# Sinkhorn normalisation of two batches with one row or column per partition, and the other two batches' chain placed later

## The chip, the core and the metric

The kernel runs on one core of a Trainium2 chip. Its metric is the device time of one execution in microseconds; three runs were taken, and one more execution was profiled. Engines are named as in the profile: PE (TensorE, the matrix engine), DVE (VectorE), ACT (ScalarE), POOL (GpSimd) and SP (SyncE, which here only starts DMAs).

## The reference

Four batches, 8 heads, 768 positions, head dimension 64. Each sequence is cut into 8 blocks of 96. A small 8 x 8 matrix per batch and head (`sort_net`) is turned into a soft permutation by five rounds of exp, division by row sums and division by column sums (Sinkhorn). It mixes the blocks of k and v; attention then runs block by block, and the result goes through a feed-forward network with squared ReLU.

```python
for _ in range(5):
    P = P - np.max(P, axis=-1, keepdims=True)
    P = np.exp(P)
    P = P / (np.sum(P, axis=-1, keepdims=True) + 1e-09)
    P = P / (np.sum(P, axis=-2, keepdims=True) + 1e-09)
k_sorted = np.einsum('bhij,bhjcd->bhicd', P, k_b)     # v the same way
scores = scale * np.matmul(q_b, k_sb.transpose(0, 1, 2, 4, 3))
attn = softmax(scores)                                # over the 96 keys of one block
x = np.matmul(attn, v_sb)                             # (3072 tokens, 512)
h = np.maximum(x @ w_in, 0.0)                         # 512 -> 2048
out = h * h @ w_out                                   # 2048 -> 512
```

## The kernel before

**Order.** Nothing is left to a scheduler of the framework. The kernel lists its operations in a planner (`Plan`), each with an engine, a cost in microseconds and what it depends on; `Plan.run` plays the list through in time, and the operations are issued on each engine in the order in which they began there. Each engine then works strictly in that order. On PE there are two lists, attention and feed-forward; an attention operation is taken when it is ready before the next feed-forward piece, or when its due number (the table `DUES`, counted in feed-forward pieces) has come. `FIRST` is the order of batch 0's first half, written by hand: K, V (sorting k, v), S (scores), T (turning v), A (attention times v), X (turning the output), F (first pieces of the feed-forward); an upper-case letter evicts on ACT, a lower-case one on DVE. The costs and dues of the planner are constants in the kernel.

**Sinkhorn.** `p_sb` holds the 32 matrices (4 batches x 8 heads), one per partition, 64 numbers each. One iteration is an exp on ACT (L465) and six DVE instructions: reduce, reciprocal and multiply along rows, and the same along columns (L409 to L416). After the fifth, `p_last` multiplies once more into bf16 and transposes 32 x 32 (L424), and `p_spread` (L489) multiplies with a 0/1 matrix `sel`, so that each partition (j, c) holds P[i, j] of every head. `build_w` (L501) multiplies this with a 0/1 mask into `w_all`, the 128 x 128 weights with which k and v are sorted on PE (`s_sort`, L628; for the second halves of batch 0 `s_sort2`, L664). Some further small instructions on `xT` (L448, L452, L456) run each kind of instruction once, and their results are not used. While PE has nothing to do in this stage, `fill` (L438) gives it matmuls on `ones`.

**The rest.** Batch 0 is done in two halves, so that feed-forward work can begin early. Batches 1 to 3 sort k and v in another layout, by small matmuls with `w_t` (`build_wt`, L526 and L533; `s_nat`, L784), which needs P of all batches. V goes through DRAM and back (`v_way`, L808 and L814). Scores are L699, their exp L719 and L728, attention times v L890, its normalisation L900 and L901. Each feed-forward unit takes 384 tokens: 16 groups of four matmuls up (L1012), ReLU on ACT (L1020), square on DVE (L1023), and 48 matmuls down in groups of four (L1042).

**Loads.** POOL issues nearly all of them (L324): q of batch 0 (heads 4 to 7), k and v of batch 0 by pairs of heads, `w_in` in four parts, `w_out` in four parts, then v, k and q of batch 1. SP issues the other half of batch 0's q (`q32`, as fp32, cast on ACT at L473), and ACT `sort_net`. POOL also builds the identity, the masks and a part of `w_all` between its loads.

Of the kernel before, what the change touches and what calls it, by code (L numbers as in the profile page):

```python
# [8 lines left out]
FP32 = mybir.dt.float32  # L9
# [12 lines left out]
    (0, "K"): (-242.5, -237.0, -449.5, -391.0),  # L22
    (0, "S"): (-214.5, -217.0, -359.5, -370.5),
    (0, "T"): (-167.5, -226.5, -373.0, -268.5),
    (0, "A"): (-159.0, -195.0, -306.0, -99.0),
    (0, "X"): (-124.0, -130.5, -290.5, -94.5),
    (0, "W"): (-245.5,),
    (1, "V"): (-115.0, -110.5),
    (1, "Q"): (-94.0,),
    (1, "N"): (None, -50.5),  # L30
    (1, "Z"): (None, None, 33.5, 34.0),
    (1, "S"): (-53.0, -3.0, 38.5, 51.0),
    (1, "A"): (-45.5, 3.5, 45.5, 51.0),
    (1, "X"): (43.5, 24.5, 56.0, 53.5),
    (2, "L"): (60.0,),
    (2, "N"): (66.5, 69.5),
    (2, "V"): (63.5, 79.5),
    (2, "Z"): (77.5, 81.5, 85.5, 81.5),
    (2, "S"): (80.0, 84.0, 102.5, 97.0),
    (2, "A"): (82.0, 86.0, 102.5, 98.0),  # L40
    (2, "X"): (90.5, 118.0, 111.0, 114.0),
    (3, "L"): (123.0,),
    (3, "N"): (132.0, 141.0),
    (3, "V"): (128.0, 138.5),
    (3, "Z"): (133.5, 133.5, 149.5, 143.0),
    (3, "S"): (147.0, 153.0, 161.0, 158.0),
    (3, "A"): (147.0, 154.5, 162.0, 158.5),
    (3, "X"): (156.5, 161.5, 195.0, 182.0),
# [4 lines left out]
FIRST = ("K0' v0 K1 v1 S0 t0' S1 t1' A0 K2' V2 A1 K3 S2 t2' v3' S3 x1' A2 T3' x0 A3 X2' F1 F0 "  # L53
         "F4 F3 F7 F6 X3")
# [130 lines left out]
def kernel(  # L185
# [60 lines left out]
    def copy(eng, out, in_):  # L246
        if eng == "ACT":
            nc.scalar.copy(out=out, in_=in_)  # L248
        else:
# [14 lines left out]
    p_sb = const.tile([NH, NB, NB], FP32)  # L264
    nc.scalar.dma_start(out=p_sb, in_=sort_net.rearrange("b h i j -> (b h) i j"))
    xT = const.tile([128, d_model // 128, B * S], BF16)
    q32 = [xT[:, 1 + g, 2 * S:].bitcast(FP32).rearrange("p (h x) -> p h x", h=2)
           for g in range(2)]
    for g in range(2):
        nc.sync.dma_start(out=q32[g], in_=q_r[0, :, 2 * g:2 * g + 2, :])  # L270
# [5 lines left out]
    nc.vector.memset(ident, 0.0)  # L276

# [35 lines left out]
    w_out_bf = const.tile([128, NT, d_model], BF16)  # L313
    w_all = const.tile([128, H + HP, NB, C0], BF16)
# [6 lines left out]
    def dma(key, mb, dst_src, deps=(), long=True, rate=0.23):  # L321
        def issue(e):
            dst, src = dst_src()
            nc.gpsimd.dma_start(out=dst, in_=src)  # L324
        op = plan.add("POOL", 0.75, issue, deps)
        landed[key] = plan.add("DMA", mb / (0.39 if key[0] == 0 else 0.43 if long else rate), lambda e: None, [op, landed.get("last")])
        landed["last"] = landed[key]
# [25 lines left out]
    first = plan.add("DMA", 3.95, lambda e: None)  # L353
# [3 lines left out]
    id_op = plan.add("POOL", 0.4, lambda e: make_identity(nc, ident, nomemset=True))  # L357
# [41 lines left out]
    rs = const.tile([NH, NB], FP32)  # L399
    cs = const.tile([NH, NB], FP32)  # L400
    pf = const.tile([NH, NB, NB], BF16)
    sel = xT[0:32, 0, 3 * S:3 * S + 32 * C0].rearrange("p (j c) -> p j c", c=C0)
    pt = const.tile([128, NB, NH], BF16)
    p_ij = const.tile([NH, 2, NH], BF16)

    def sink_norm(e, axis, last=False):
        view = p_sb if axis == 0 else p_sb.transpose([0, 2, 1])
        r = rs if axis == 0 else cs
        nc.vector.reduce_sum(out=r, in_=view, axis=AX.X)  # L409
        nc.vector.reciprocal(out=r, in_=r)  # L410
        if last:
            return
        nc.vector.tensor_tensor(
            out=p_sb, in0=p_sb,
            in1=(r[:, :, None] if axis == 0 else r[:, None, :]).to_broadcast([NH, NB, NB]),
            op=ALU.mult)  # L416

    def p_last(e, k):

        i = slice(NQ * k, NQ * (k + 1))  # L420
        nc.vector.tensor_tensor(
            out=pf[:, i, :], in0=p_sb[:, i, :],
            in1=cs[:, None, :].to_broadcast([NH, NQ, NB]), op=ALU.mult)
        nc.vector.transpose(out=p_ij[:, k, :],  # L424
                            in_=pf[:, i, :].rearrange("h i j -> h (i j)"))
# [16 lines left out]
    t32 = xT[:, 3, 2 * S:].bitcast(FP32)  # L442
    nc.vector.memset(t32[:, 0:136], 1.0)

    def warm(e):
        fill(2.4, 0)
        for n in range(2):
            nc.tensor.matmul(out=p2[1][:, 0, 8 * n:8 * n + 8], lhsT=t32[:, 0:128],  # L448
                             rhs=t32[:, 128:136], start=True, stop=True)

    def try_exp(e):
        nc.scalar.activation(out=t32[:, 144:152], in_=t32[:, 128:136], func=AF.Exp,  # L452
                             accum_out=t32[:, 152:153])

    def try_rec(e):
        nc.vector.reciprocal(out=t32[:, 160:168], in_=p2[1][:, 0, 8:16])  # L456


    plan.add("PE", 4.3, warm, [plan.add("DVE", 1.1, lambda e: None)])

    exps, casts = [], []
    step = plan.add("SP", 2.25, lambda e: None)
    step0 = step
    for it in range(5):
# [3 lines left out]
        if it == 0:  # L468
            plan.add("ACT", 0.3, try_exp, [step])
# [750 lines left out]
```

## Time and profile before

| | |
|---|---|
| median of three runs | 219.02 us (218.44 to 220.64) |
| the profiled execution | 218.59 us, of which 216.8 us between first and last instruction |
| granted PE clock, mean | 0.998 |
| PE busy | 209.8 us, 97% of the span |
| DVE, ACT, POOL busy | 109.9, 121.4, 28.4 us |
| HBM read, written | 29.70 MB, 8.72 MB |
| matmuls up, L1012 | 506, 88.1 us |
| matmuls down, L1042 | 368, 84.6 us |

The span is cut by the profile into 40 slices of 5.4 us; digits give the busy share of an engine in tenths. Matmuls overlap and their ends are modelled, so PE's share is not a share of peak. The chain of work that ended last is followed back from the last instruction, each step to what released it. A line number is that of the kernel printed above; one line can hold the copies of many stages (L248 on ACT, L250 on DVE).

### The profile page before, as it was taken

How to read it: one execution, taken by the hardware profiler on the slowest of the kernel's cores; microseconds unless marked ns; L12 is line 12 of the kernel's file. 1: busy time of each engine (PE TensorE's matmuls, PEld its weight loads, DVE VectorE, ACT ScalarE, POOL GpSimd, SP SyncE). 2: the span in 40 equal slices, each digit the busy share in tenths (PEclk: the TensorE clock that was granted, in tenths of full speed). 3: DMA queues.
4: the chain of work that ended last, by engine and by line, in shares of the span. 5: the costliest groups of instructions: out<-in, count | busy, mean ns of one | idle time of the engine just before them, and what ended most of it. 6: DMA issues, size and time to landing. Idle time of an engine off the chain costs nothing.

```text
span 216.8 us, 5097 instructions
## 1 busy us (share of the span) xinstructions
PE 209.8 (97%) x2040; PEld 116.1 (54%) x2040; DVE 109.9 (51%) x300; ACT 121.4 (56%) x252; POOL 28.4 (13%) x53
## 2 busy tenths in 40 slices
PE   8898999799999999999999999999999999999994
PEld 3466765346655555445665455445655565456542
DVE  4778576345894447643895045517675154015300
ACT  5777985227783268436774177328865375147421
POOL 7994320000000700000000330000000000000000
PEclk9999999999999999999999999999999999999999
DMA  6999999999968799939852599599884310120012
GB/s 183 194 204 207 206 208 209 194 173 292 225 125 76 136 211 228 188 102 194 187 153 64 121 192 215 105 208 229 98 209 115 91 48 3 48 97 0 0 51 97
DMA packets 47864, 31.92 MB, mean 147 GB/s; under 512 B 27296, under 2 KB 42912, under 8 KB 47840
## 3 DMA queue, kind: packets, MB, share of 16 engines
q1 hardware_dynamic: 35568, 18.34, 37.8%
q0 software_dynamic: 12224, 13.24, 37.8%
q8 instruction: 16, 0.26, 0.5%
q14 instruction: 8, 0.07, 0.1%
q10 hardware_dynamic: 48, 0.01, 0.0%
HBM read 29.70 MB, written 8.72 MB: 177 GB/s over the span
## 4 chain that ended last, share of the span: by engine, by line
PE 81%; DMA 14%; POOL 3%; issue 1%; ACT 0%; POOLq 0%
PE op L1042 36%; PE hp L1012 34%; DMA vb<-in_v_dram 9%; DMA w_in_bf<-in_moe_w_in_dram 5%; PE p L890 3%; PE p L699 3%; PE p L784 2%; PE op L1070 2%; POOL vb L324 1%; POOL kb L324 1%; POOL qb L324 1%; PE qtp L578 0%; PE p L628 0%; PE xtp L943 0%; POOL ident masks.py:199 0%
## 5 line engine op out<-in xcount | busy, mean ns | idle before, releaser
L1012 PE MATMUL hp<-xT,w_in_bf 128*128 128x384 bf16 x506 | 88.1, 326 | 0.0
L1042 PE MATMUL op<-w_out_bf,h 128*128 128x512 bf16 x368 | 84.6, 379 | 0.0
L1020 ACT ACTIVATE h<-hp 128x384 bf16<-128x384 f32 x128 | 61.7, 495 | 17.8 <-PE hp L1012 14.7
L1023 DVE TENSOR_TENSOR h<-h 128x384 bf16<-128x384 bf16 x128 | 43.6, 354 | 44.2 <-ACT h L1020 43.8
L1012 PEld LDWEIGHTS <-w_in_bf 128*128 128x128 bf16 x506 | 47.3, 98 | 31.2 <-issue 0.7
L1042 PEld LDWEIGHTS <-h 128*128 128x128 bf16 x368 | 33.9, 98 | 38.3 <-issue 1.2
L248 ACT COPY ob<-op 128x512 f32<-128x512 f32 (+2 forms) x23 | 13.1, 568 | 48.7 <-PE op L1042 46.3
L728 ACT ACTIVATE et<-p 96x384 bf16<-96x384 f32 x48 | 19.7, 488 | 9.3 <-PE p L699 9.3
L901 DVE TENSOR_TENSOR ao<-p,rec 96x512 bf16<-96x512 f32 x32 | 22.0, 686 | 1.3 <-DVE rec L900 0.2
L890 PEld LDWEIGHTS <-et 96*128 96x128 bf16 x256 | 11.7, 97 | 5.2 <-issue 0.7
L250 DVE CAST vn<-p 128x768 bf16<-128x768 f32 x6 | 5.7, 958 | 15.1 <-PE p L784 10.7
L900 DVE RECIPROCAL rec<-p 96x8 f32<-96x8 f32 x32 | 6.4, 201 | 10.3 <-PE p L890 8.7
L1159 POOL COPY held<-xT 1x3 bf16<-1x3 bf16 (+1 forms) x2 | 0.4, 186 | 85.8 <-DMA xT<-ao 85.8
L248 ACT CAST vn<-p 128x768 bf16<-128x768 f32 x6 | 4.8, 800 | 9.1 <-PE p L784 9.1
L890 PE MATMUL p<-vblk,et 96*128 96x65 bf16 x192 | 9.6, 193 | 0.0
L438 PE MATMUL p<-ones 128*128 128x512 bf16 (+1 forms) x28 | 8.5, 433 | 1.1 <-DVE ones L274 1.1
L699 PEld LDWEIGHTS <-kvT 64*128 64x128 bf16 x256 | 6.2, 94 | 5.4 <-issue 3.1
L844 DVE COPY kvT<-kx 128x768 bf16<-128x768 bf16 x10 | 8.4, 847 | 0.0
L250 DVE CAST kn<-p 128x768 bf16<-128x768 f32 x5 | 4.8, 956 | 5.5 <-PE p L784 5.5
L324 POOL DMA_DIRECT2D kb<-in_k_dram x10 | 6.5, 646 | 4.1 <-DMA w_out_bf<-in_moe_w_out_dram 1.8
L324 POOL DMA_DIRECT2D vb<-in_v_dram x10 | 6.3, 630 | 3.0 <-DMA w_in_bf<-in_moe_w_in_dram 3.0
L324 POOL DMA_DIRECT2D qb<-in_q_dram x8 | 6.0, 750 | 2.7 <-DMA w_in_bf<-in_moe_w_in_dram 1.9
(88 smaller groups left out, 120.0 us busy)
## 6 DMA issues: line engine op xcount, KB each, us to landing
out_dram<-ob SPq DMA_DIRECT2D x23, 256.0 KB, 3.2
v_way<-vn SPq DMA_DIRECT2D x6, 396.0 KB, 5.3
vblk<-v_way SPq DMA_DIRECT2D x6, 396.0 KB, 4.1
vb<-in_v_dram POOLq DMA_DIRECT2D x6, 384.0 KB, 11.9
kb<-in_k_dram POOLq DMA_DIRECT2D x6, 384.0 KB, 10.4
qb<-in_q_dram POOLq DMA_DIRECT2D x6, 384.0 KB, 13.4
w_in_bf<-in_moe_w_in_dram POOLq DMA_DIRECT2D x4, 512.0 KB, 11.1
w_out_bf<-in_moe_w_out_dram POOLq DMA_DIRECT2D x4, 512.0 KB, 16.3
```

Of the source, the lines that this page charges most:

```text
L248: nc.scalar.copy(out=out, in_=in_)
L250: nc.vector.tensor_copy(out=out, in_=in_)
L324: nc.gpsimd.dma_start(out=dst, in_=src)
L438: nc.tensor.matmul(out=p2[slot][:, 0, 0:128 * r].rearrange("p (r x) -> p r x", r=r), lhsT=ones, rhs=ones[:, None, :].to_broadcast([128, r, ...
L699: nc.tensor.matmul(out=scp[:, h, BLK * n:BLK * (n + 1)], lhsT=u.ksT[64 * h:64 * (h + 1), HS * hf + BLK * n:HS * hf + BLK * n + 128], rhs=( ...
L728: nc.scalar.activation(out=et[:, h, 0:HS].rearrange("p (n c a) -> p n c a", c=C0, a=NA), in_=st["p"][0:96, h, 0:HS].rearrange("p (n a c) - ...
L890: nc.tensor.matmul(out=oup[:, h, 66 * n:66 * n + D + 1], lhsT=et_r[u.et[hf]][:, h, BLK * n:BLK * n + 128], rhs=(u.vs[:, NQ * hf + n, h, 0: ...
L901: nc.vector.tensor_tensor(out=u.ao[:, n0:n0 + NQ, :, :].rearrange("p n e d -> p e n d"), in0=ov[:, :, :, 0:D], in1=rec[:, :, :, None].to_b ...
L1012: nc.tensor.matmul(out=t["hp", nt][:, 0:HS], lhsT=w_in_bf[:, kc, 128 * nt:128 * (nt + 1)], rhs=xT[:, kc, t0:t0 + HS], start=(kc == 0), sto ...
L1020: nc.scalar.activation(out=t["h1", nt], in_=t["hp", nt][:, 0:HS], func=AF.Relu)
L1023: nc.vector.tensor_tensor(out=t["h2"][:, nt, :], in0=t["h1", nt], in1=t["h1", nt], op=ALU.mult)
L1042: nc.tensor.matmul(out=t["op", mt], lhsT=t["h2"][:, nt, 128 * mt:128 * (mt + 1)], rhs=w_out_bf[:, nt, :], start=(nt == 0), stop=(nt == NT ...
```

## The change

The two first batches (16 heads, 128 rows of 8) get a tile of their own, `p_a`, with one matrix row per partition. The row sum of the first iteration comes with the exp (`accum_out`). `widen` writes the normalised rows as a block-diagonal 128 x 128 matrix, and an fp32 matmul with `by_i` turns it: from there on a partition holds a column. In iterations 1 to 4 the exp takes the column's reciprocal as its scale; an fp32 matmul with the block matrix `blk` adds the rows up over partitions; `by_columns` multiplies by the reciprocal and gives the column sum in the same instruction. At the end one bf16 matmul with `spread` takes the place of transposes and eight small matmuls, and both first `w_all` builds read its PSUM tile.

The last two batches keep the old form on 16 partitions (`p_sb`, `late_norm`), five iterations issued one by one among the feed-forward work, and `late_spread` puts them into `pt` ahead of `build_wt`. `sort_net` is now loaded by SP, `p_a` first, then `q32`, then `p_sb`. `make_identity` stands ahead of the first loads on POOL; the unused instructions are gone; the fill ahead of the chain is shorter. `pt` holds heads and rows in the other order. `DUES`, `FIRST`, the engines of the first query copies and the planner's numbers for loads are set anew.

```diff
-FIRST = ("K0' v0 K1 v1 S0 t0' S1 t1' A0 K2' V2 A1 K3 S2 t2' v3' S3 x1' A2 T3' x0 A3 X2' F1 F0 "
-         "F4 F3 F7 F6 X3")
+FIRST = ("k0' V0 k1 V1 S0 t0' S1 t1' A0 K2 V2' A1 K3 S2 t2' v3 S3 X0 A2 T3' X1' X2' A3 F0 F1 F3 "
+         "F4 F6 F7 x3")
...
-    p_sb = const.tile([NH, NB, NB], FP32)
-    nc.scalar.dma_start(out=p_sb, in_=sort_net.rearrange("b h i j -> (b h) i j"))
+    p_a = const.tile([128, NB], FP32)
+    nc.sync.dma_start(out=p_a, in_=sort_net[0:HA // H].rearrange("b h i j -> (b h i) j"))
...
+    make_identity(nc, ident, nomemset=True)
...
+    for g in range(2):
+        nc.sync.dma_start(out=q32[g], in_=q_r[0, :, 2 * g:2 * g + 2, :])
+    p_sb = const.tile([HL, NB, NB], FP32)
+    nc.sync.dma_start(out=p_sb, in_=sort_net[HA // H:].rearrange("b h i j -> (b h) i j"))
...
+    def widen(dst, src, r):
+        nc.vector.scalar_tensor_tensor(
+            out=dst.rearrange("p (h i) -> p h i", i=NB),
+            in0=src[:, None, :].to_broadcast([128, HA, NB]), scalar=r,
+            in1=by_h[:, :, None].to_broadcast([128, HA, NB]), op0=ALU.mult, op1=ALU.mult)
+
+    def by_columns(src, with_):
+        nc.vector.scalar_tensor_tensor(
+            out=ph, in0=src, scalar=1.0, in1=with_, op0=ALU.mult, op1=ALU.mult,
+            accum_out=sums[:, 2:3])
+        nc.vector.reciprocal(out=sums[:, 3:4], in_=sums[:, 2:3])
...
     def warm(e):
-        fill(2.4, 0)
-        for n in range(2):
-            nc.tensor.matmul(out=p2[1][:, 0, 8 * n:8 * n + 8], lhsT=t32[:, 0:128],
-                             rhs=t32[:, 128:136], start=True, stop=True)
+        fill(1.7, 0)
...
+    def chain_step(it):
+        if it == 0:
...
+            exps.append(plan.add("ACT", 0.3, lambda e: nc.scalar.activation(
+                out=e_a, in_=p_a, func=AF.Exp, accum_out=sums[:, 0:1]), [step]))
+            def rows(e):
+                nc.vector.reciprocal(out=sums[:, 1:2], in_=sums[:, 0:1])
+                widen(wide, e_a, sums[:, 1:2])
...
+                nc.tensor.matmul(out=chain["p"][:, 0, :], lhsT=wide, rhs=by_i,
+                                 start=True, stop=True)
...
+            chain["ph"] = plan.add("DVE", 0.48, lambda e: by_columns(chain["p"][:, 0, :], one8), [pe])
+        else:
+            exps.append(plan.add("ACT", 0.2, lambda e: nc.scalar.activation(
+                out=e_a, in_=ph, func=AF.Exp, scale=sums[:, 3:4]), [chain["ph"]]))
+            pe = plan.add("PE", 0.22, lambda e: nc.tensor.matmul(
+                out=chain["p"][:, it, :], lhsT=blk, rhs=e_a, start=True, stop=True), exps[-1:])
+            def norm(e):
+                nc.vector.reciprocal(out=rr, in_=chain["p"][:, it, :])
+                by_columns(e_a, rr)
...
+    def p_spread(e):
+        t = tiles["pt_ps"] = psf.tile([128, HA, NB], FP32, tag="pf", name="pt_ps")
+        nc.tensor.matmul(out=t.rearrange("p h i -> p (h i)"), lhsT=spread, rhs=wide_b,
+                         start=True, stop=True)
+
+    def late_chain(after):
+        plan.add("ACT", 0.6, make_sel, after)
+        step = plan.add("DVE", 0.1, lambda e: nc.vector.memset(pf, 0.0), after)
+        for it in range(5):
+            step = plan.add("ACT", 0.2, lambda e: nc.scalar.activation(
+                out=p_sb, in_=p_sb, func=AF.Exp), [step])
+            for axis in range(2):
+                for n in range(3):
+                    step = plan.add("DVE", 0.2, lambda e, axis=axis, n=n, it=it: late_norm(
+                        e, axis, n, it == 4 and axis == 1), [step])
...
+    def late_spread(due):
...
+                    out=st["p"][:, i, :],
+                    lhsT=sel[:, NB * (i % 4):NB * (i % 4 + 1), :].rearrange("p j c -> p (j c)"),
+                    rhs=p_ij[:, i // 4, 0:HL], start=True, stop=True)
...
+        pe = plan.add("PE", 0.28, mm, [chain["late"]] + old, due, mode="col32")
+        chain["pt"] = plan.add("DVE", 0.3, lambda e: nc.vector.tensor_copy(
+            out=pt[:, HA:NH, :].rearrange("p h i -> p i h"), in_=st["p"]), [pe])
...
+    chain["late"] = late_chain([landed["w_in", 2]])
```

On PE, 64 matmuls up and 8 down stood ahead of the first L784 (sorting batch 1's v); in the changed program 64 up and 28 down stand there, and the late matmuls (`late_p`) and those of `build_wt` between them.

## Prediction

> **What bounds the kernel now.** I read the page first, then the chain of work that ended last, then busy times by stretch, then the timeline of the first 23 us. The page says that TensorE is the engine of this kernel.
>
> ```profile
> span 216.8 us, 5097 instructions
> ...
> PE 209.8 (97%) x2040; PEld 116.1 (54%) x2040; DVE 109.9 (51%) x300; ACT 121.4 (56%) x252; POOL 28.4 (13%) x53
> ...
> PE   8898999799999999999999999999999999999994
> ```
>
> But the 97% holds matmuls on `ones` (L438) that only fill time, and those lie in the first 13 us. The chain of work tells the rest: up to 39.03 us it runs through loads, from there on through TensorE alone.
>
> ```profile
> 8.65 9.96 DMA w_in_bf<-in_moe_w_in_dram
> 18.61 0.28 issue
> 18.89 20.09 DMA vb<-in_v_dram
> 38.98 0.04 issue
> 39.03 0.39 PE p L784 x16
> 39.41 4.42 PE op L1042 x20
> ```
>
> The busy times by stretch (TensorE is the second number after the length) put a size on it: 1.40 us with no matmul just before that load lands, none lost in the 174.62 us after it.
>
> ```profile
> 21.50:37.63 16.13, 16.13 (x240) 10.47 (x238) 10.54 (x27) 13.10 (x25) 3.46 (x6) 1.00 1.22 208
> 37.63:39.03 1.40, 0.01 (x2) 0.00 (x1) 0.00 (x0) 0.00 (x0) 0.00 (x0) 1.00 1.07 199
> 39.03:213.65 174.62, 174.61 (x1468) 93.69 (x1468) 83.88 (x202) 93.50 (x194) 7.63 (x14) 1.00 0.68 136
> ```
>
> So the end is: when TensorE starts its real work (the second-half sort, L664, at 21.51 us), plus its work, plus 1.40 us of wait. The Sinkhorn chain that the change rewrites stands ahead of all of it. Its first and last links, from the timeline:
>
> ```profile
> 2.98 0.26 ACT L465 ACTIVATE p_sb<-p_sb 32x64 f32<-32x64 f32 x1 [0.49 <-DMA p_sb<-in_sort_net_dram]
> ...
> 3.14 0.19 ACT L452 ACTIVATE xT<-xT 128x8 f32<-128x8 f32 x1
> ...
> 3.24 0.18 ACT L452 ACTIVATION_READ_ACCUMULATOR xT<-xT 128x1 f32 x1
> ...
> 3.51 0.19 DVE L410 RECIPROCAL rs<-rs 32x8 f32<-32x8 f32 x1
> ...
> 4.55 0.63 PEld L448 LDWEIGHTS p<-xT 128*128 128x128 f32 x4
> ...
> 4.76 0.51 PE L448 MATMUL p<-xT 128*128 128x8 f32 x4
> ...
> 4.81 0.25 ACT L465 ACTIVATE p_sb<-p_sb 32x64 f32<-32x64 f32 x1
> ```
>
> ```profile
> 12.21 0.47 PE L489 MATMUL pt_ps<-p_ij,xT 32*128 32x32 bf16 x8
> ...
> 12.59 0.29 DVE L501 TENSOR_TENSOR w_all<-mask,pt_ps 128x128 bf16<-128x128 bf16 x1 [0.23 <-PE pt_ps L489]
> ```
>
> The five exponentials start at 2.98, 4.81, 6.57, 8.33 and 10.09 us: 1.78 us an iteration, six VectorE instructions each. The first `w_all` is built at 12.59.
>
> **The new chain, link by link.** The load `p_a` is first on its queue as `p_sb` was, with half the bytes in rows of 32 B: I keep the 2.2 us to landing of `p_sb`, so 2.98. Iteration 0: exp with accumulator 0.28 (the two L452 rows, 3.14 to 3.42), hop 0.03, reciprocal 0.19, gap 0.03, `widen` 0.25, hop 0.10, fp32 matmul 0.45, hop 0.08, multiply with sum 0.20, gap 0.03, reciprocal 0.19, hop 0.05: 1.88 us. Iterations 1 to 4: exp 0.19, hop 0.05, matmul 0.45, hop 0.08, reciprocal 0.19, gap 0.03, multiply 0.20, gap 0.03, reciprocal 0.19, hop 0.05: 1.46 us each. Then `widen` and its gap 0.28 (less the last hop), and 0.35 for one bf16 matmul with its hops. Sum: 2.98 + 1.88 + 4 x 1.46 - 0.05 + 0.28 + 0.35 = 11.28 us for the first `w_all`, 1.31 earlier than 12.59.
>
> Not in the trace are `scalar_tensor_tensor` with a sum, `widen`, and one fp32 matmul alone. The multiply lies between 0.14 (L421, 32x32) and 0.25 (the column reduce); I take 0.20, nearer the other small VectorE rows of 0.19 to 0.21. `widen` lies between 0.17 (memset of 128x136) and 0.42 (L501, 128x256); 0.25, as 128x128 takes 0.29 in bf16 with one operand more by stride. The two L448 matmuls took 0.72 in all (4.55 to 5.27), so one is between 0.36 and 0.72; 0.45, half plus the tail of a pass. An exp is 0.19 to 0.26. With all low an iteration is 1.31 us, with all high and hops of 0.10 it is 2.0, slower than now: `w_all` at 10.6 or at 13.8.
>
> One rule speaks against these links. The Trainium skill, "ScalarE: Activation LUTs", section "What ACT_TABLE_LOAD costs", says that an activation with a per-partition pointer as its scale takes about 93 ns more; L452 has an immediate scale, so no row here shows it. By that rule four exponentials would cost 0.37 us more, and the build would come at 11.65.
>
> A second one: the ten fills at 1.06 us took 3.87 us (0.39 each), seven at 7.76 took 1.58 (0.23 each), though the granted clock reads 1.00 in both. "TensorE: Matmul & The Clock Gate", section "What's actually happening", has the array at half clock until about 3.4 us of sustained work, and back there after an idle window. The new order has 17 fills for 28; by that rule a chain run cold would pay some 0.2 us in each of five matmuls. I see no pause near 3.4 us in the order and leave it out.
>
> **What reaches the second-half sort.** I walked the new order from a build at 11.4. Both builds now read PSUM on VectorE (0.29 each, no wait for ScalarE's copy, which had put the second at 13.21), so the four sorts end near 12.6 instead of 14.1. But ScalarE evicts both V tiles and one more transposed query ahead of the first attention exp, which starts at 13.4 instead of 14.44, and takes the turned outputs X0 and X1 (0.48 each) that VectorE had. The last attention matmul of that group comes at 19.0 instead of 19.73, L664 at 20.6 instead of 21.51: **0.9 us** of the 1.3. Loads would allow it. `make_identity` (0.31 on POOL) now stands ahead of the two query loads, and the SP queue issues `p_a` (0.44) ahead of `q32`: all loads move by about 0.4 us. `w_in` part 0 landed 10.0 after its issue at 8.65, so 19.05 now, when the first FFN piece is ready for it; the last V tile of batch 0 has 0.5 us of room. If these covers are gone, each 0.1 us of load is 0.1 us of start.
>
> **The wait of 1.40 us** goes. Before the first L784 now stand 28 down matmuls, not 8. Their 20 x 0.216 = 4.33 us were done after 39.03 before; now they fill the time until V of batch 1 lands (39.4), so TensorE arrives at 41.8 and the load is covered by 2.3 us. The DRAM round trip of V that follows starts that much later: its attention stands at 59.2 against 58.43, and the round trip (write at 40.58, read back at 52.57, 4.1 us to landing) then has about 1.5 us of room, the batch-1 query load (lands 46.75 + 0.4) the same.
>
> **What is added on TensorE.** Eight matmuls for the late 16 rows: 0.28. Coming back from a small-tile mode costs 0.10 each time (op x4 0.97 against 0.865 in the chain); before L784 that is four more returns, 0.4. After it there are three more, 0.3, and score groups of 8 in place of 16 (0.28 twice against 0.45, two more pairs), 0.2. Sum **1.2 us**.
>
> **The late chain** itself is 30 VectorE links of 0.24 and five exponentials of 0.35 with hops, with two transposes: 9.3 us, off TensorE, between 24 us (its place in the order) and the matmul `late_p` at 39.3. Cover: TensorE's 24 up and 20 down matmuls. But VectorE and ScalarE, busy 10.54 and 13.10 of 16.13 us in that stretch, get 7 and 1.9 us more, and the chain's last nine links stand behind the last square. That square comes 1.1 to 2 us after the last up matmul (34.9); the tail takes 2.9; so `late_p` is ready between 38.9 and 39.9. Queued behind it on TensorE are `wtp`, L784 and everything else. I allow **0.2 us**.
>
> **Sum**, on the profiled execution's own 218.59 us (span 216.8 and 1.8 around it): 218.59 - 0.9 - 1.4 + 1.2 + 0.2 = 217.7. The median of the three runs is 0.43 above that execution; I go half of it up: **217.9 us**.
>
> **Rivals.** (1) *The start gains all of it.* If the links run at their low ends and the returns cost nothing beyond `late_p`, the sort starts 1.4 us earlier: 218.59 - 1.4 - 1.4 + 0.5 = 216.3. For it: most small VectorE rows are pure overhead, alike for 8 and 64 elements. Against: ScalarE's added evictions. (2) *The chain is no shorter*: matmul 0.72, exp 0.26, queued neighbours (a query copy of 0.46 stands in VectorE's queue between links twice). At 1.78 us an iteration nothing is gained at the start: 218.59 - 1.4 + 1.2 + 0.2 = 218.6, no change. For it: an engine hop more per iteration. Against: four instructions fewer on VectorE. (3) *Slower: the late chain holds TensorE at `late_p`.* Its 36 links are in order with 16 relus and 16 squares. From 24.5 to 39.3 it has 14.8 us for 9.3, so 0.15 us a link may be lost; above 0.18 the kernel is slower than before, and at 0.30 (most links behind one square of 0.35) the chain ends at 44.6, 5.3 us late: 217.5 + 5.3 = 222.8. For it: two engines near full. Against: the links stand spread through the order, not in a block, and relus and squares have rings of three.
>
> **How the numbers follow.** Forecast 0.50 (217.0 to 218.6), rival 1 0.24, rival 2 0.13, rival 3 0.13. About 1%, 2.2 us, is what a measurement of this kernel can tell from no change: faster is below 216.8, which is most of rival 1 and the low edge of the forecast, 0.29; slower is above 221.2, most of rival 3, 0.10; the rest 0.61. The range reaches from 215.9 (rival 1 with a start 1.8 us earlier) to 220.3 (rival 3 with 0.23 us lost a link: 24.5 + 9.3 + 8.3 = 42.1, 2.8 late).
>
> **What would show it.** Right: exponentials 1.4 to 1.55 us apart, `w_all` near 11.4, L664's successor near 20.6, no TensorE wait at L784's successor, which starts near 41.8. Wrong: a TensorE wait ahead of `late_p` on VectorE; exponentials 1.8 apart; TensorE idle for V's way back or for the batch-1 query load; or a stretch after L784 longer than 171 us.

## The result, and the profile after

The changed kernel took 221.52 us (median of four runs, 220.2 to 222.49) beside 219.04 us of the kernel before (218.44 to 220.64): a ratio of 1.0113, with a 95% interval of 1.0076 to 1.0149. It is slower by about 1%; the forecast was 217.9 us, no change. The profiled execution took 220.2 us with a span of 218.4 (before: 218.59 and 216.8). All ratios in this document leave out executions more than 1.5% above the fastest of their kernel, medians and ranges do not, so that the two can lean apart.

The page of the profile after, as it was shown of before, with the row of the granted clock besides:

```profile
span 218.4 us, 5099 instructions
...
PE 210.9 (97%) x2020; PEld 117.1 (54%) x2036; DVE 112.4 (51%) x327; ACT 121.7 (56%) x254; POOL 28.2 (13%) x53
...
PE   7798999999999999999999999999999999999994
...
PEclk9759999999999999999999999999999999999999
```

VectorE has 27 instructions more, TensorE's share is as it was; the first two slices (11 us) read 77 where they read 88 before, and the clock, which read 9 in every slice before, reads 7 and 5 in the second and third.

The end of the kernel is still when the second-half sort starts on TensorE (L738, formerly L664) plus its work. The busy times by stretch of the profile after, with TensorE second after the length, show where the time lies. The stretches are cut at L738 and at the sort of batch 1's v (L858, formerly L784).

```profile
1.00:22.77 21.77, 19.39 (x322) 12.85 (x323) 12.73 (x62) 13.64 (x29) 17.44 (x30) 0.84 1.16 201
22.77:43.84 21.07, 21.02 (x268) 12.45 (x268) 16.91 (x66) 13.89 (x30) 2.90 (x5) 1.00 1.24 200
43.84:215.28 171.44, 170.49 (x1434) 91.81 (x1448) 82.59 (x199) 93.64 (x194) 7.62 (x14) 1.00 0.66 135
```

TensorE has next to no idle time in the last two lines (0.05 us, and at most 0.95, as some matmul records are missing): the wait of 1.40 us for V is gone. The granted clock stands behind the busy times: 0.84 in the first stretch, 1.00 in the others. So most of the miss is in the start: the sort came at 22.77, against 21.51 before and 20.6 in the prediction. From the sort to the last instruction it is 195.7 us (195.6 to 195.7 in e2, e5 and e7 too), against 195.3 before. The wait that was saved there went into added work, and the change could gain only by an earlier sort.

The same view, cut into four pieces of 3.41 us, says what the clock did there. (3.41 us is the shortest time between two changes of the clock in this record.)

```profile
1.94:5.35 3.41, 3.20 (x11) 1.32 (x9) 1.27 (x7) 0.77 (x5) 3.41 (x6) 1.00 0.92 255
5.35:8.76 3.41, 2.64 (x47) 1.84 (x47) 1.67 (x10) 2.33 (x6) 2.83 (x5) 0.99 1.25 189
8.76:12.17 3.41, 3.06 (x62) 2.15 (x62) 2.02 (x11) 1.90 (x5) 2.64 (x9) 0.50 1.31 201
12.17:15.58 3.41, 3.41 (x78) 2.50 (x76) 1.68 (x4) 2.13 (x5) 3.41 (x6) 0.50 1.30 203
```

For 6.8 us, from 8.7 to 15.6, TensorE had half its clock. There was no pause ahead of it: in the 3.41 us before the fall TensorE was busy for 2.64. In the kernel before the same stretch has 1.00 throughout:

```profile
5.30:8.70 3.40, 2.77 (x56) 1.56 (x56) 2.53 (x14) 2.24 (x6) 3.40 (x6) 1.00 1.29 191
8.70:12.10 3.40, 3.40 (x59) 1.70 (x57) 2.70 (x14) 2.66 (x8) 3.08 (x10) 1.00 1.31 199
12.10:15.50 3.40, 3.31 (x88) 2.49 (x88) 2.47 (x8) 2.61 (x7) 3.40 (x6) 1.00 1.29 203
```

The timeline of the profile after has the links of the chain (start, length, engine, line; in brackets the idle time before, and what ended it).

```profile
2.57 0.21 ACT L483 ACTIVATE e_a<-p_a 128x8 f32<-128x8 f32 x1 [0.55 <-DMA p_a<-in_sort_net_dram]
...
3.10 0.35 DVE L431 SCALAR_TENSOR_TENSOR xT<-e_a,sums,by_h 128x128 f32<-128x128 f32 x1
...
4.02 0.43 PE L494 MATMUL rows<-by_i,xT 128*128 128x8 f32 x2
...
4.49 0.17 DVE L437 SCALAR_TENSOR_TENSOR ph<-rows,one 128x8 f32<-128x8 f32 x1 [1.04 <-PE rows L494]
...
4.97 0.30 ACT L500 ACTIVATE e_a<-ph,sums 128x8 f32<-128x8 f32 x1 [2.10 <-DVE sums L440]
...
6.53 0.30 ACT L500 ACTIVATE e_a<-ph,sums 128x8 f32<-128x8 f32 x1 [0.54 <-DVE sums L440]
...
10.00 0.59 PE L502 MATMUL rows<-e_a,xT 128*128 128x8 f32 x2 [0.35 <-ACT e_a L500]
...
12.16 0.29 DVE L575 TENSOR_TENSOR w_all<-mask,pt_ps 128x128 bf16<-128x128 bf16 x1 [0.45 <-PE pt_ps L527]
...
12.78 0.29 DVE L575 TENSOR_TENSOR w_all<-mask,pt_ps 128x128 bf16<-128x128 bf16 x1 [0.33 <-ACT pt L1185]
```

The exponentials stand 1.56 us apart (4.97, 6.53), not 1.46; the first iteration took 2.40 (2.57 to 4.97), not 1.88, because the turning matmul, with its operand written at 3.45, began at 4.02, when the fills were through; and the second build still waits for ScalarE's copy `pt` of the same PSUM tile.

### The profile page after: what moved, and what is told of

It is laid out like the page before. It is cut to its first block, busy times and chain, and to the rows that moved or that the text cites. A ratio compares the mean times of both kernels' runs of the same rounds, so it can differ in the third digit from the quotient of the medians.

```text
span 218.4 us, 5099 instructions
## 1 busy us (share of the span) xinstructions
PE 210.9 (97%) x2020; PEld 117.1 (54%) x2036; DVE 112.4 (51%) x327; ACT 121.7 (56%) x254; POOL 28.2 (13%) x53
## 3 DMA queue, kind: packets, MB, share of 16 engines
q0 software_dynamic: 12224, 13.24, 37.0%
## 4 chain that ended last, share of the span: by engine, by line
PE 93%; DVE 3%; ACT 2%; issue 1%; DVEq 0%; ACTq 0%
PE hp L1086 38%; PE op L1116 36%; PE p L964 4%; PE p L773 4%; PE p L466 2%; PE p L858 2%; PE op L1144 2%; PE qtp L652 1%; DVE ao L975 1%; PE vbp L822 1%; PE p L738 1%; PE tp L702 1%; PE xtp L1017 1%; PE rows L502 1%; ACT e_a L500 1%
## 5 line engine op out<-in xcount | busy, mean ns | idle before, releaser
L1116 PE MATMUL op<-w_out_bf,h 128*128 128x512 bf16 x352 | 83.3, 379 | 0.9 <-issue 0.2
L248 ACT COPY ob<-op 128x512 f32<-128x512 f32 (+2 forms) x24 | 13.6, 567 | 51.3 <-PE op L1116 48.8
L964 PEld LDWEIGHTS <-et 96*128 96x128 bf16 x256 | 11.2, 97 | 4.2 <-issue 0.5
L466 PE MATMUL p<-ones 128*128 128x512 bf16 (+1 forms) x17 | 6.7, 500 | 1.1 <-DVE ones L271 1.1
L793 ACT ACTIVATE et<-p 96x768 bf16<-96x768 f32 x8 | 6.3, 802 | 0.7 <-PE p L773 0.6
```

The lines of the kernel that those rows point to most:

```text
L466: nc.tensor.matmul(out=p2[slot][:, 0, 0:128 * r].rearrange("p (r x) -> p r x", r=r), lhsT=ones, rhs=ones[:, None, :].to_broadcast([128, r, ...
L964: nc.tensor.matmul(out=oup[:, h, 66 * n:66 * n + D + 1], lhsT=et_r[u.et[hf]][:, h, BLK * n:BLK * n + 128], rhs=(u.vs[:, NQ * hf + n, h, 0: ...
L1116: nc.tensor.matmul(out=t["op", mt], lhsT=t["h2"][:, nt, 128 * mt:128 * (mt + 1)], rhs=w_out_bf[:, nt, :], start=(nt == 0), stop=(nt == NT ...
```

## The experiments

The times of all of them, each with the runs of the kernel before on the same chip:

| kernel | median (range, executions) | before | ratio, 95% interval |
|---|---|---|---|
| e1 | 221.5 (221.15 to 221.8, 4) | 219.14 | 1.0109, 1.0092 to 1.0125 |
| e2 | 219.98 (219.12 to 223.2, 10) | 219.14 | 1.0028, 1.0011 to 1.0045 |
| e3 | 219.75 (218.74 to 221.65, 12) | 219.14 | 1.0023, 0.9996 to 1.0050 |
| e4 | 222.41 (220.84 to 224.12, 6) | 219.14 | 1.0153, 1.0111 to 1.0195 |
| e5 | 219.16 (218.62 to 219.83, 12) | 219.34 | 0.9977, 0.9949 to 1.0004 |
| e6 | 222.71 (219.59 to 224.06, 12) | 219.34 | 1.0055, 1.0008 to 1.0102 |
| e7 | 219.77 (219.16 to 224.37, 12) | 219.34 | 0.9996, 0.9963 to 1.0030 |
| e8 | 221.31 (219.68 to 223.87, 12) | 219.34 | 1.0072, 1.0033 to 1.0110 |
| e9 | 219.4 (218.86 to 223.05, 12) | 219.49 | 0.9999, 0.9969 to 1.0029 |
| e10 | 222.0 (220.88 to 222.88, 6) | 219.49 | 1.0111, 1.0068 to 1.0155 |
| e11 | 221.84 (221.63 to 222.06, 2) | 219.49 | 1.0105, 1.0034 to 1.0175 |
| e12 | 219.21 (218.74 to 219.57, 10) | 219.2 | 0.9982, 0.9949 to 1.0015 |
| e13 | 219.94 (219.33 to 224.16, 14) | 219.21 | 1.0018, 1.0003 to 1.0032 |
| e14 | 219.43 (219.18 to 224.06, 10) | 219.21 | 0.9996, 0.9967 to 1.0024 |
| e15 | 220.28 (219.19 to 222.76, 12) | 219.21 | 1.0044, 1.0012 to 1.0076 |

### The clock of the start: e1, e2, e3, e10

e1 is the changed kernel once more.

> The changed kernel as it is, a second time, to see what differs between its executions (the four known ones span 220.2 to 222.5 us; those of the kernel before 218.4 to 220.6). Clock theory: the first matmuls of the second-half sort (L738) start anywhere between 22.5 and 25 us, by how long the array runs at half clock in the first 16 us; everything after that is alike to 0.5 us. Rival (the links of the new chain and the order of the evictions cost what is missing, the clock is a by-product): the start at L738 is 22.8 again to 0.2 us, and the spread lies in later waits.

Its profiled execution took 221.8 us and put the sort at 23.72, almost 1 us later than the other. The granted clock reads 1.00 all the way, yet the matmuls tell otherwise: at 9.15 us the fp32 matmul took what it takes at half clock.

```profile
9.15 0.60 PE L502 MATMUL rows<-e_a,xT 128*128 128x8 f32 x2
```

In the first profile it took 0.39 at 5.32, with the clock at 1.00, and 0.59 at 10.00, with the clock at 0.50. In e1 it took 0.60 from its first use at 5.32 to its last: this execution was slow from its first matmul until about 16 us, and the granted clock showed nothing of it. The clock record of e1 has its first entry at 16.65 us, and the view counts the time ahead of a first entry as full clock.

e2 gives TensorE denser fills between the links:

```diff
-            if filled and not started and op.gap > 0.15 and slot is not None:
-                fill(op.gap - (0.5 if op in pes else 0.05), slot)
+            if filled and not started and op.gap > 0.1 and slot is not None:
+                fill(op.gap - (0.05 if op in pes else 0.0), slot)
```

> The changed kernel with the gaps that fill() gets in the chain not cut by 0.5 us but by 0.05 us, some eight 128x512 matmuls on ones more. Clock theory: the granted clock stays at 1.00 from 8 to 15 us (0.50 without), the sort L738 starts at 21.3 us (22.8 without), and the time falls by 1.4 us or more against the changed kernel, to about 219. Rival (links and eviction order): the clock may come back, but the chain is bound by ScalarE and VectorE, L738 stays at 22.4 or later, and the time moves by less than 0.5 us.

It gained 1.5 us at the median (221.5 to 219.98), and the intervals of the two ratios lie apart. Its trace kept 1.00 through the stretch in which the changed kernel had 0.50:

```profile
5.35:8.76 3.41, 2.56 (x31) 1.51 (x31) 1.25 (x9) 1.29 (x3) 1.68 (x3) 1.00 1.22 185
8.76:12.17 3.41, 3.08 (x83) 2.16 (x80) 2.05 (x10) 2.40 (x7) 2.72 (x5) 1.00 1.30 199
```

The sort at 21.3 that the clock theory asked for was not seen: in that execution ScalarE waited 1.09 us for a late q, so its sort came at 22.66 all the same. So the gain is told by the medians, and by one stretch of the trace: from the first `w_all` to the first scores it took 1.68 us (13.01 to 14.69), where the changed kernel, in the same order, took 2.36 (12.16 to 14.52).

e10 goes the other way and leaves out all fills between the links (`if False:` in place of the first line).

> The changed kernel without any fill between the links of the chain (the first seven stay). Theory A, the clock of the start is what the thinner fills lost: half clock from the chain on in every execution, until the attention work is dense (near 16 us), and 221.5 to 222.5, like the changed kernel or slower. Rival B, the fills cost more by standing in front of the chain's matmuls than they bring: 220.0 to 220.5.

222.0, as the clock theory had it. The busy times by stretch show the fall at 7.5, and the way back three windows later:

```profile
4.09:7.50 3.41, 1.75 (x43) 1.43 (x41) 1.24 (x10) 2.04 (x4) 3.15 (x6) 0.99 1.22 235
7.50:10.91 3.41, 2.21 (x48) 1.89 (x44) 2.01 (x10) 1.71 (x5) 2.10 (x4) 0.50 1.30 193
...
14.32:17.73 3.41, 3.41 (x64) 2.73 (x58) 1.75 (x5) 2.61 (x5) 3.41 (x6) 0.51 1.26 203
17.73:21.14 3.41, 2.64 (x65) 2.12 (x64) 2.54 (x6) 2.75 (x6) 2.30 (x4) 1.00 1.24 208
```

The earlier fall is not the work of the missing fills alone: by the clock records the first full clock came at 4.0 us here and at 5.3 in the changed kernel, and in both the fall came one window later.

e3 thins out the fills of the kernel before (each chain fill to 0.35 of its length):

```diff
-                fill(op.gap - (0.5 if op in pes else 0.05), slot)
+                fill(0.35 * (op.gap - (0.5 if op in pes else 0.05)), slot)
```

> The kernel before with the fills inside the chain cut to about a third (18 fills to 6 in the chain; the first ten stay). Clock theory: the granted clock falls to 0.50 somewhere between 7 and 16 us, the sort L664 starts 0.7 to 2 us later than 21.5, and the time rises by as much. Rival: fills only pass time; the time stays within 0.3 us.

The executions spread from 218.74, the time of the fastest of the kernel before beside it, to 221.65. At the median that is no change that can be told. The slowest was profiled: half clock from 9.31 to 26.40, five windows.

```profile
9.31:26.40 17.09, 16.05 (x282) 12.44 (x282) 10.49 (x33) 9.78 (x21) 10.85 (x20) 0.50 1.26 205
```

The time follows the mean clock of the execution. Where it was 1.00 they took 218.84 and 218.86 us; at 0.984, which works out as two such windows at half clock, 218.74 to 219.4; at 0.976 and 0.977, three, 219.63 and 219.92; at 0.969, four, 219.86 to 220.78; at 0.961, five, 221.65. So the old chain loses at most 0.6 us by two windows at half clock, and nearly 3 us by five. The later kernels say the same by count: of the 50 executions of e7, e9, e13 and e15, 13 had a mean clock of 0.968 to 0.984 and took 221.6 to 224.4 us; the other 37 had 0.997 or more and took 218.9 to 220.9.

### The order of the attention work: e4, e5

e4 puts the new `DUES` and the new planner numbers for loads into the kernel before, with its old chain, old `FIRST` and old load order.

> The kernel before with its old chain for all four batches, but the load model and the table of dues of the changed kernel (order of work after the first stage alone). My step for the wait: 24 down matmuls stand ahead of the first sort of batch 1's v instead of 8, so the 1.40 us wait for that load goes, and 0.4 us comes back in returns from small-tile modes: 1.0 us less than before, about 218.0. Rival: what is saved there comes back as another wait later (v's way through memory, the query load), and the time stays at 219.

222.41, slower than either. Its profiled execution was at half clock up to 13 us (sort at 24.83), and it had a wait of 1.1 us for a turned output late in the kernel that neither kernel has. The wait for V was gone here too, with 24 down matmuls ahead of it. The run mixes the clock and the order and tells little of the dues; it shows no gain from the new order.

e5 is e2 with the old `FIRST`:

```diff
-FIRST = ("k0' V0 k1 V1 S0 t0' S1 t1' A0 K2 V2' A1 K3 S2 t2' v3 S3 X0 A2 T3' X1' X2' A3 F0 F1 F3 "
-         "F4 F6 F7 x3")
+FIRST = ("K0' v0 K1 v1 S0 t0' S1 t1' A0 K2' V2 A1 K3 S2 t2' v3' S3 x1' A2 T3' x0 A3 X2' F1 F0 "
+         "F4 F3 F7 F6 X3")
```

> The changed kernel with the denser fills of e2 (median 219.98 there), and the order FIRST of the kernel before. In e2's trace the stretch from the first scores (14.69) to the second-half sort (22.66) is 7.97 us, in the kernel before 7.46, with waits for ao (the normalised output, DVE) that the kernel before does not have. Theory A, the new FIRST costs this stretch: 7.5 us again, the time 0.5 lower, 219.5. Rival B, the stretch is set by the late loads and by ACT's evictions, whatever the order: 220.0, stretch near 8. Rival C, the new order suits the new chain, the old one puts its evictions into the chain's engines: slower, 220.5.

219.16, and no execution above 219.83; the interval of its ratio lies below that of e2. The stretch from the first scores (14.05) to the sort (21.72) is 7.67 us; it was 7.97 in e2 and 8.25 in the changed kernel (14.52 to 22.77). The chain of work of the changed kernel shows what the order does there (start, length, what):

```profile
18.11 0.70 DVE ao L975
...
18.85 0.35 PE p L773 x8
19.19 0.28 PE xtp L1017 x4
19.47 0.27 PE p L964 x8
...
20.07 0.70 DVE ao L975
...
20.81 0.34 PE xtp L1017 x4
21.15 0.27 PE p L964 x8
...
21.75 0.70 DVE ao L975
...
22.50 0.34 PE xtp L1017 x4
```

Three normalisations (`ao`, DVE) follow one another, each with a turn and the next attention matmul behind it: the new order has X2 ahead of A3, so the last attention matmul of the group stands behind a turn that waits for the normalisation before it. In e5 the same view has one normalisation, and A3 stands ahead of X2.

### The chain's own links: e7, e12

e7 is e2 with one fill fewer ahead of the turning matmul and the second build ahead of the copy:

```diff
-        fill(1.7, 0)
+        fill(1.45, 0)
...
     w0 = build_w(0, 2, None, pes[-1], 0, NQ)
+    w1 = build_w(2, 2, None, pes[-1], 0, NQ)
     cp = plan.add("ACT", 0.27, lambda e: nc.scalar.copy(
-        out=pt[:, 0:HA, :], in_=tiles["pt_ps"]), pes[-1:])
-    w1 = build_w(2, 2, None, pes[-1], 0, NQ)
+        out=pt[:, 0:HA, :], in_=tiles["pt_ps"]), [w1])
```

> e2 with two trims of the chain: the first fill is 6 matmuls instead of 7 (the matmul that turns the rows stood behind the fills until 4.02 with its operand ready at 3.45), and the second w_all build goes ahead of ACT's copy of the same PSUM tile (it waited for that copy, about 0.3). Theory A, these are links that I mis-sized: first exponential after the turn 0.35 earlier, second build 0.3 earlier, together 0.5 off the time, 219.5. Rival B, the start is set by the query loads, not by the chain: no change, 220.0. Rival C, one fill less and the clock is half again in more executions: 220.5 or more.

The turning matmul began at 3.60, and the first scores came at 13.24, 0.8 earlier than in the kernel before: this is what the new chain can do. The end did not follow. With the new `FIRST` the sort came 8.42 us later, at 21.66, and the time is that of the kernel before. A part of that stretch is a load: v of the third pair of heads landed 8.9 us after its issue at 6.28, and TensorE's weight loads for its sort waited 0.3 us.

e12 makes the exponential's scale a constant, which leaves the column division out of four iterations.

```diff
-                out=e_a, in_=ph, func=AF.Exp, scale=sums[:, 3:4]), [chain["ph"]]))
+                out=e_a, in_=ph, func=AF.Exp), [chain["ph"]]))
```

> e7 with a constant as the scale of the four later exponentials of the chain instead of the column's reciprocal read from a tile (the division by column sums is left out of iterations 1 to 4). In e7's trace such an exponential takes 0.30 us and they stand 1.56 us apart; the first one, with a constant, takes 0.21. Theory A, the operand is on the chain's path: exponentials of 0.21, 1.47 apart, the first scores 0.36 earlier (12.9 for 13.24); at the end of the kernel 0.0 to 0.3, because the loads of k and v of batch 0 are near (219.1 to 219.4 for e7's usual 219.4). Rival B, the spacing is set by VectorE's links or by what stands on TensorE's queue: 1.56 again, 219.4.

The exponentials took 0.21 instead of 0.30 and from the second to the fourth stood 1.33 to 1.40 apart; the last stood at 8.78, not 9.22. And the first scores came at 13.27, no earlier. The view of VectorE's waits between 10 and 12.5 us names the next floor:

```profile
DVE w_all L575 <- POOL mask L375: 1.1, 1, 1.1
```

The build needs the 0/1 `mask`, which POOL makes behind its loads. In the changed kernel POOL waits 0.53 us for the landing of q (0.6 to 1.8 in the kernels built on it) before it can issue the next load, and the mask is ready at 11.2; the kernel before had no such wait and had it at 10.5. In e7 VectorE's first build already waited 0.4 us for POOL. In the changed kernel itself this floor was hidden: the chain came later than it.

### The loads: e6, e8, e14

e6 is e2 with `p_a` issued by ACT, so that `q32` is first on SP; e8 is e5, e6 and e7 together.

```diff
-    nc.sync.dma_start(out=p_a, in_=sort_net[0:HA // H].rearrange("b h i j -> (b h i) j"))
+    nc.scalar.dma_start(out=p_a, in_=sort_net[0:HA // H].rearrange("b h i j -> (b h i) j"))
```

> e2 with the load of p_a issued by ACT instead of SP, as the kernel before issues p_sb: q32 is then first on SP's queue and is issued 0.46 us earlier. In e2's trace ACT's second query cast waits 1.09 us for q32 and holds the exponential behind it to 9.14. Theory A, the place of p_a ahead of q32 costs the start: casts without a wait, 219.5. Rival B, when these loads land differs from execution to execution by more than 0.46 us, and the chain rarely waits for them: 220.0, no change. Rival C, ACT's own issue (0.44) puts off its table load and the first exponential by 0.4: 220.3.

> e5, e6 and e7 together on e2. Theory A, the three are separate costs and add: 219.98 - 1.4 = 218.6, ahead of the kernel before by about 0.5. Rival B, they cover each other (the later of chain and loads decides): 219.3, like the kernel before. If the clock at the start decides alone: 220.0.

None of e6's three theories had it. The first exponential, which waits for `p_a`, stood at 3.58 us (3.54 in e8) instead of 2.4 to 2.6: issued at the same time on the other queue, `p_a` landed 1 us later with `q32` going out beside it. The place that the change gave it, first on SP, was worth that 1 us. Without it SP's second part of q landed at 5.5 us (6.6 in the changed kernel, 6.1 in e7), and ScalarE did not wait for it in either run; POOL's part came no earlier, and POOL's wait for it was 1.0 us in e8. Seven of e6's twelve executions took over 222.6 us; the profiled one ran its matmuls at half speed up to 19 us.

e14 is e7 with a second load of the same 128 rows of 32 bytes, on ACT's queue, into a tile that nothing reads.

> e7 with a second load of the same 128 rows of 32 bytes into a tile that nothing reads, issued by ACT at the start. Theory A, the 128 small rows of p_a (the old p_sb had 32 rows of 256 bytes) hold up the DMA engines and with them q, k and v: q lands another 0.3 to 0.5 us later, POOL's wait for q grows from 0.68 to 1.1 or more, the mask comes at 11.6 or later, and the time is 219.6 to 220. Rival B, small rows cost nothing, the loads are later because they are issued later: POOL's wait 0.7 again, first exponential 0.1 to 0.4 later because ACT issues a load first, 219.4.

POOL's wait grew from 0.68 to 0.92 and the first scores went from 13.24 to 13.34: between the two theories, and within what single executions differ by. What makes q land later is not settled.

### The late chain: e11

Four of the five late iterations are left out, the plan's times kept:

```diff
-            step = plan.add("ACT", 0.2, lambda e: nc.scalar.activation(
+            step = plan.add("ACT", 0.2, lambda e, it=it: it < 4 or nc.scalar.activation(
...
-                    step = plan.add("DVE", 0.2, lambda e, axis=axis, n=n, it=it: late_norm(
+                    step = plan.add("DVE", 0.2, lambda e, axis=axis, n=n, it=it: it < 4 or late_norm(
```

> The changed kernel with four of the five iterations of the late chain left out (24 small instructions on VectorE and four exponentials on ScalarE less; the last two batches are mixed with weights of one iteration), in the same order otherwise. My step, the late chain is hidden behind TensorE's work: the stretch from the second-half sort to the sort of batch 1's v stays at 21.0 to 21.1 us, the time within 0.2 of the changed kernel in executions with the same start. Rival, the added 7 us of VectorE work slow the relus and squares and so TensorE: the stretch 20.5 or less.

The stretch from the sort (23.41) to the sort of v (44.47) is 21.06 us, the same as 21.07 with all five. The four iterations cost nothing where they stand.

### What is left when all is repaired: e9, e13, e15

e9 is e7 with the old `FIRST`.

> The changed kernel with the denser fills (e2), the two trims of the chain (e7) and the order FIRST of the kernel before (e5), but p_a left first on SP's queue. In e7's trace the first scores stand at 13.24 and the second-half sort at 21.66, 8.42 later; with the old order (e5) that stretch was 7.67. Theory A, start of the chain and order of the first half are two separate costs: sort at 20.9, and with the 195.7 us that every execution of the changed kernel took from the sort to the end, a span of 216.6 and a time of 218.4, ahead of the kernel before by 0.3 to 0.6. Rival B, something else (w_in, the POOL builds of w_all for the second half) holds the sort near 21.6 once the chain is early: 219.2, like e5 and e7.

219.4, a ratio of 0.9999: rival B. The old `FIRST` is all that e9 changes in e7 (0.9996), so here the order was worth nothing, and its stretch from the first scores to the sort was 8.34 us, as long as e7's 8.42. Its profiled execution had lost 0.45 in the chain (four fills at half clock ahead of the second matmul), first scores 13.62, and 0.48 us of idle TensorE ahead of the sort of the third pair's v; the profile names no load there, so I call the cause open.

e13 takes the mask off POOL; e15 has one fill fewer as well.

```diff
-        src, w = ident, 64
+        src, w = mask, 8
...
+    with nc.allow_low_precision("sums of zeros and one 1"):
+        nc.vector.reduce_sum(out=mask, in_=ident.rearrange("p (w c) -> p c w", c=C0), axis=AX.X)
```

> e9 with the 0/1 mask of build_w made by one VectorE reduction ahead of the chain (about 0.4 us, in a gap of 0.55) instead of three POOL additions behind the loads; POOL then has 1.0 us less ahead of w_in's later parts. In the changed kernels POOL waits 0.5 to 1.1 us for the landing of q (in the kernel before it does not wait there) and the mask is ready at 11.2 to 11.9, where the kernel before had it at 10.5; in e12 the first build waited 1.06 us for it. Theory A, the mask is the next floor under the start: no VectorE wait for POOL at the first build, second-half sort some 0.3 us earlier than e9's 21.96, 219.1. Rival B, the floor is v of the third pair of heads (e9: 0.48 us wait ahead of that sort): sort where it was, 219.4.

> e13 with three fills instead of four ahead of the chain's second matmul (in e9's trace four of them ran at half clock until 5.54 and that matmul, ready at 4.9, stood behind them: exponentials 2.05 apart there, 1.56 elsewhere). Theory A, the chain is then 0.3 to 0.45 earlier in executions that are still cold there, 218.8. Rival B, loads of v decide: like e13.

Neither was a gain. VectorE no longer waited for POOL. e13's profiled execution still had its sort at 22.18, no earlier than e9's 21.96; e15's had the earliest sort of all the changed versions, 21.41. In both, TensorE waited for a load or for v's way back later on. The view of TensorE's waits after 22 us, of e13 and then of e15:

```profile
PE op L1118 <- DMA w_out_bf<-in_moe_w_out_dram: 0.7, 1, 0.7
```

```profile
PE p L966 <- DMA vblk<-v_way: 0.3, 1, 0.3
```

The down matmuls that the change moved ahead of the sort of v need `w_out`, and in e13 they waited for it: its last part landed 22.4 us after its issue, against 20.2 in e9. And with one fill fewer, 5 of e15's 12 executions fell to half clock, against 4 of 14 in e13 and 2 of 12 in e9, which is too few to tell them apart. No version beat the kernel before by more than can be told; e5 comes nearest.

## Why the prediction was wrong, step by step

**The clock step fell.** The sentence "I see no pause near 3.4 us in the order and leave it out" is the first that failed, and the largest that the runs show. Between the forecast of 217.9 us and the median of 221.52 lie 3.6 us. By e1 and e2 the clock is 1.5 of them; e5 takes off another 0.8 with the old `FIRST`; for the remaining 1.3, which no run takes apart, the terms of the chain and of the stretch after the sort are below. I had both halves in hand: the fills at 0.39 and 0.23 us in one profile, and the rule of the Trainium skill ("TensorE: Matmul & The Clock Gate", section "What's actually happening"). No pause was needed: the clock fell after a window in which TensorE was busy for 2.64 of 3.41 us, with no gap above 0.46. The stretches at half clock last 6.8 us here, 10.2 in e10 and 17.1 in e3, which are two, three and five times 3.41. My price by that rule, 0.2 us in each of five matmuls, was too small as well, because everything from 8.7 to 15.6 us ran so, the first four sorts among it (0.32 us each instead of 0.21). It is probably also why the median (221.52) lies above the profiled execution (220.2), which fell for two windows only; the others were not profiled. On the skill's page, in sentences of their own: its window of about 3.4 us agrees with these lengths. That section has the fall come after an idle window, and in the changed kernel a thin one was enough.

**The chain sum was short by 0.88 us** (12.16 for 11.28; before 12.59), by its own terms. The load came 0.41 earlier than I had it: `p_a` is first on SP, and with `q32` beside it in e6 it came 1 us later. Iteration 0 took 0.52 more: from `widen` to the matmul 0.92 instead of 0.35, by the fills at half clock and by 0.10 on `widen` itself. Three periods took 0.30 more (1.56 for 1.46): the exponential 0.11, the reciprocal `rr` and the gap behind it 0.09, less 0.10 for the matmul, which was quicker than my 0.45. The last stage took 0.47 more, with the matmul at half clock and again 0.10 on `widen`. `by_columns`, which no row had shown, was right: 0.21 to the instruction after it, where I had 0.23. The skill's page "ScalarE: Activation LUTs", section "What ACT_TABLE_LOAD costs", was right where I took the row: 93 ns by the page, 0.30 against 0.21 measured.

**"0.9 us of the 1.3" fell by more than all of it.** From the first build to the sort I had 9.32 us (11.28 to 20.6); it took 10.61. e5, which kept its clock and has the old order, took 9.35 (12.37 to 21.72). So the difference divides in two. From build to scores it is 0.68 (2.36 us against 1.68), which is the half clock, as e2 took 1.68 with the new `FIRST`. From scores to sort it is 0.58 (8.25 against 7.67). By e2's 7.97 about half of that is the new `FIRST`; the rest I put down to the half clock, which lasted 1 us beyond the first scores. These are single executions, and e9 took 8.34 with the old `FIRST` (0.48 of it idle), so the share of the order is not settled. I had walked that order for ScalarE's evictions and not for VectorE's normalisations, which stand three deep in it. The second build's wait for ScalarE's copy, which I had declared gone, is still there, but costs nothing: build to scores is 1.66 in e7, without it.

**The rest held.** The wait of 1.40 us went, as told. From the sort to L858 I had 21.2 us, and 21.07 was measured; the late chain was ready without a wait of TensorE for it, and e11 shows that four of its iterations cost nothing, so rival 3 fell. The stretch after it is 171.4 where I said at most 171, and 170.8 by the sum: 0.6 more, which no run took apart. Rival 2, a chain no shorter, was nearest, but by luck: the chain was shorter by 0.43 us, and the start was lost behind it. Sum: 217.7, and 2.17 at the start, less 0.13, and 0.6, is 220.3; the profiled execution took 220.2.

**What I missed besides** is POOL's queue. I moved "all loads by about 0.4 us" and asked only whether their readers had room; the instructions behind POOL's new wait, the mask among them, were readers too. It cost nothing here, but it is the floor that e7 and e12 ran into; v of the third pair of heads in e7 was another. The 1.40 us of the old profile were a sign of it: TensorE there was already ahead of a load.

## What to carry to other kernels

When a change thins out the work of TensorE in a latency-bound stage, price the whole stage at half clock as well and let that be the upper end: a window of small matmuls was enough to lose it here, it was then gone for two to five windows, and matmul lengths told it where the clock record did not. Fills there are a balance: at half clock they held the next link by 0.45 us (e9), and thinner ones or none lost the clock (e3, e10). And before a start is made earlier, ask which load ends last behind it: in e12 the mask, which waits in POOL's queue behind a load, took the whole gain.

## What was not expected of the hardware

- The granted clock can read 1.00 from the start of a profile even where the matmuls run at half speed: in e1 the fp32 matmul took 0.60 us throughout, where 0.39 is its length at full clock, and the view showed 1.00 to the end.
- The share of busy time does not tell when the clock falls: 2.64 of 3.41 us busy came before a fall in the changed kernel, 2.56 in the same stretch of e2 did not. The first full clock came at 5.3 us in the one and at 6.8 in the other, so the windows do not lie alike. What the hardware counts cannot be read from these rows.
- Two engines did not read one PSUM tile at the same time in these kernels: in both, ScalarE's copy began when VectorE's first build had ended, and in the changed kernel VectorE's second build waited 0.33 us for that copy. (In the kernel before, the second build reads the copy itself.) In e7 the two builds stand ahead of the copy, and it began behind them. Whether the chip or the program's waits ask for it was not tried.
